# Pooled attention and a gelu MLP on one core: a weight sum, K's spread, an operand sum and a query load put elsewhere in a hand-written order

## The chip, the cores and the metric

The kernel runs on one core of a Trainium2 chip. The metric is the device time of one execution in microseconds (us), as the median of several. Five engines work side by side: TensorE (PE in the profile, with PEld for its weight loads), VectorE (DVE), ScalarE (ACT), GpSimd (POOL) and SyncE (SP), which here only issues DMAs. Each takes its instructions in the order in which the program gives them, so an instruction that waits holds up everything behind it on its engine.

## The reference

Attention over pooled keys and values, and then an MLP with gelu:

```python
B, H, S, D = q.shape                      # 8, 8, 576, 64
k_p = k.reshape(B, H, S // 8, 8, D).mean(axis=3)     # 72 keys a head
v_p = v.reshape(B, H, S // 8, 8, D).mean(axis=3)
scores = scale * np.matmul(q, k_p.transpose(0, 1, 3, 2))
attn = np.exp(scores - np.max(scores, axis=-1, keepdims=True))
attn = attn / (np.sum(attn, axis=-1, keepdims=True) + 1e-09)
x = np.matmul(attn, v_p)                  # then transposed to (B*S, H*D) = (4608, 512)
h = x @ w_in                              # 512 -> 2048
g = 0.5 * h * (1.0 + np.tanh(c * (h + 0.044715 * h * h * h)))
out = g @ w_out                           # 2048 -> 512
```

## The kernel before, in words

The 4608 rows are worked in nine groups of 512. Eight groups are the first 512 queries of a batch each; the ninth, called R (the remainder), gathers the last 64 queries of all eight batches. The order is `seq` = 0, 1, ..., 6, R, 7, and a group's turn is called a step here, numbered by its place in `seq`: step 7 is R, step 8 is batch 7.

A step is the MLP of its group on TensorE. Into the same stretch the attention of the next group is woven, and the loads of the one after. Step 0 has its own form, `mlp_first`. In the others `mlp` makes the hidden layer in 64 places (0 to 63; `hidden_two` at L526 and `hidden` at L379 in steps 1 and 2, and from step 3 on, where `fast` is true, `hidden_fast`, a product of Strassen's kind at L470), and then the output layer at L581 as seven half-size products in the order 1, 2, 6, 5, 7, 3, 4, with 16 matmuls each, in places 64 to 175. Product n in this order starts at place 64 + 16n.

The weaving is by hand. `at(hooks, s, f, ...)` puts a call on a list for place s, and `hook(s)` makes all calls of place s just ahead of the matmul of that place. So a call's place fixes where its instructions stand in each engine's queue; when they run depends on what they wait for. Calls of one place are made in the order in which they were put there.

The parts that the change touches:

- `w_sums` (L423): four sums of pieces of `w_out`, made once into `tw` by VectorE, 128x2048 each. Number 0 stands at place 185 of step 0, numbers 1 to 3 in the first places of step 1. Products 5, 6, 7 and 4 use them.
- `values` (L338, for R L349): the product of weights and V, and the casts of its result to `xT`, the input of the next step's hidden layer. It stands late in every step, at place 186 in step 0. In step 0 and step 1 two casts of 128x1024 are made, one by ScalarE and one by VectorE.
- `g_sums` (L430 to L434): sums of blocks of the gelu output `gT`. Its lines L430 to L432 (which 0) make s3, a block in place, and s2; L434 (which 1) makes s4, the fourth operand. Product 6 reads s2, product 7 s3, product 3 s4.
- `k_spread` (L94 through `copy`, written `kbd<-kTd`): two copies of the transposed, pooled K of the next group into `kbd`, which the scores (L244) read. `spread_v` (L172, `vbd`) does the like for V on GpSimd.
- `norm` (L260, L269, L275) makes the softmax weights `eb` from the exponentials, j = 0 and 2 on GpSimd and j = 1 and 3 on VectorE, and `e_transpose_dma` (L302) turns each of the four into `eT` by a DMA issued on SP. `values` reads `eT`: its first eight matmuls of a batch step need j = 0 and 1, the next need j = 2 and 3.
- `load_q` loads queries on SP. A batch is one DMA (L121, 1 MB). R's are gathered from all batches by eight DMAs of 128 KB (L125), in rows of 64 floats, four for `(0, 2)` and four for `(2, 4)`. The tile `q_sb` has two buffers in turn. `cast_gated` casts it on GpSimd, two steps ahead of the queries' own step.
- `load_kv` loads K and V of a group (L112, L107, L105: 2.25 MB in four DMAs, from place 28 of a step on).

Everything that SP issues stands in one queue: loads, transposes and the stores of the output (L411).

Of the kernel before, what the change touches and what calls it, by code (L numbers as in the profile page):

```python
# [19 lines left out]
def kernel(  # L20
# [21 lines left out]
    nc = tc.nc  # L42
# [10 lines left out]
    R = B  # L53
    seq = list(range(B - 1)) + [R, B - 1]
# [20 lines left out]
    NP = FO // 2  # L75
# [534 lines left out]
    def mlp_first(g, hooks):  # L610

        hook = runner(hooks)
        s = 0
        for half, c in [(0, 0), (0, 1), (0, 2), (1, 0), (0, 3), (1, 1), (1, 2), (1, 3)]:
            for fo in range(4 * c, 4 * c + 4, 2):
                hidden_half(g, fo, half, hook, s)
                s += 8
        nc.scalar.preload_act_table_set(EXP_SET)
        o = [psum.tile([128, DM], F32, name="mm", tag="mm", bufs=4) for _ in range(4)]
        for fo in range(12):  # L620
            for r in range(4):
                hook(s)
                s += 1
                output(g, r, fo, o[r])
        for r in range(4):
            for fo in range(12, FO):
                hook(s)
                s += 1
                output(g, r, fo, o[r])
            finish(g, r, o[r], nc.scalar if r == 3 else nc.vector)  # L630
        assert not hooks, sorted(hooks)
# [134 lines left out]
    def at(hooks, s, f, *a):  # L766
        hooks.setdefault(s, []).append(lambda: f(*a))

    def tail_of_attention(hooks, n, va):
        at(hooks, va, xT_tile, n)  # L770
        at(hooks, va, nc.scalar.preload_act_table_set, GELU_SET)
        at(hooks, va, values, n, False)

    hooks = {}
# [40 lines left out]
    at(hooks, 156, load_q, 2, 0, 4, nc.sync)  # L815
    at(hooks, 156, load_main, 2, "v", 0, 4, nc.sync)
    tail_of_attention(hooks, 1, 186)
    at(hooks, 185, w_sums, 0, 0, NP, nc.vector)
    mlp_first(0, hooks)

    for n_, g in enumerate(seq):
        if n_ == 0:
            continue
        hooks = {}
        fast = n_ >= 3
        if n_ == 1:
            for i in range(1, 4):
                at(hooks, i, w_sums, i, 0, NP, nc.vector)
            at(hooks, 36, g_sums, 0, 4)
            at(hooks, 57, g_sums, 4, 6)  # L830
        elif fast:
            at(hooks, 41, g_sums, 0, 2, (0,))
            at(hooks, 57, g_sums, 2, 6, (0,))
            at(hooks, 65, g_sums, 6, 8, (0,))
            at(hooks, 64 + 32, g_sums, 0, 8, (1,))
        else:
            at(hooks, 20, g_sums, 0, 2)
            at(hooks, 36, g_sums, 2, 4)
            at(hooks, 57, g_sums, 4, 6)
        if not fast:  # L840
            at(hooks, 65, g_sums, 6, 8, (0,))
            at(hooks, 64 + 32, g_sums, 6, 8, (1,))
        if n_ + 1 < len(seq):
            n = seq[n_ + 1]
            b = B - 1 if n == R else n
            kv = n != B - 1
            if n_ == 1:
                for j in range(4):
                    at(hooks, 22 + 4 * j, cast_q, n, j, j + 1, nc.scalar)
                at(hooks, 35, qT_tile, n)  # L850
                at(hooks, 35, q_transpose_dma, n)
            if kv and not fast:
                t0 = 22 if n_ == 1 else 12
                at(hooks, t0, pool, b, 0, 5)
                at(hooks, t0, dup_k, b, 0, 5)
                at(hooks, t0, kT_tile, b, None)
                at(hooks, t0, k_transpose_dma, b)
                t1 = t0 + (16 if n_ == 1 else 24)
                at(hooks, t1, pool, b, 5, 9)
                at(hooks, t1, spread_v, b, nc.gpsimd)  # L860
                at(hooks, 56, k_spread, b, [nc.vector, nc.vector])
            elif kv:
                at(hooks, 5, pool, b, 0, 5, (0,))
                at(hooks, 17, pool, b, 0, 5, (1,))
                at(hooks, 17, dup_k, b, 0, 5)
                at(hooks, 17, kT_tile, b, None)
                at(hooks, 17, k_transpose_dma, b)
                at(hooks, 17, spread_gated, b)
                at(hooks, 40, k_spread, b, [nc.gpsimd, nc.gpsimd])
            if fast:  # L870
                at(hooks, 2, qT_tile, n)
                at(hooks, 2, q_transpose_dma, n)
            sc_at = [68, 68, 90, 90]
            for j in range(4):
                at(hooks, sc_at[j], scores, n, j)
                at(hooks, sc_at[j] + 1, exps, n, j)
            at(hooks, 80, eT_tile, n)
            for j in range(4):
                at(hooks, 80 if j < 2 else 92, norm, n, j, nc.vector if j % 2 else nc.gpsimd)
                at(hooks, 80 if j < 2 else 92, e_transpose_dma, n, j)  # L880
            at(hooks, 64 + 66, nc.scalar.preload_act_table_set, GELU_SET)
            va = 64 + (102 if n_ > 1 else 100)
            at(hooks, va, xT_tile, n)
            at(hooks, va, values, n, n_ > 1)
        if n_ + 2 < len(seq):
            n2 = seq[n_ + 2]
            s2 = 44 if n_ == 1 else 8 if n2 == R else 57
            at(hooks, s2, q_tile, n2)
            if n2 == R:
                at(hooks, s2, load_q, n2, 0, 2, nc.sync)  # L890
                at(hooks, 30, load_q, n2, 2, 4, nc.sync)
            else:
                at(hooks, s2, load_q, n2, 0, 4, nc.sync)
            at(hooks, 64 + 52, cast_gated, n2)
            if n_ < 2:
                at(hooks, 64 + 100, qT_tile, n2)
                at(hooks, 64 + 100, q_transpose_dma, n2)
                at(hooks, 64 + 100, load_kv, n2, (1,))
            elif n2 != B - 1:
                b2 = B - 1 if n2 == R else n2  # L900
                at(hooks, 64 + 84, pool, b2, 5, 9, (0,))
                at(hooks, 64 + 97, pool, b2, 5, 9, (1,))
            if n_ == 1:
                at(hooks, 45, load_kv, n2, (0,))
            else:
                at(hooks, 28, load_kv, n2)
        mlp(g, hooks, n_ + 1 == len(seq), fast)
# [30 lines left out]
```

## Time and profile before

| | |
|---|---|
| Median of 8 runs | 281.6 us (280.33 to 282.18) |
| Profiled execution: time, span of the core | 281.94 us, 280.2 us |
| Granted TensorE clock | 1.000 |
| Busy: TensorE, weight loads | 269.7 us (96%), 191.9 us (68%) |
| Busy: VectorE, ScalarE, GpSimd | 224.8 us (80%), 175.7 us (63%), 71.8 us (26%) |
| DMA | 54.37 MB, 71696 packets |
| First matmul of steps 1 to 8 | 53.14, 82.55, 110.86, 138.52, 166.32, 195.54, 223.84, 251.39 us |

The times in a profile's rows are microseconds from the start of the span. A row of the timeline gives start, duration, engine, line of the kernel, operation, the tiles written and read, their shapes, and how many instructions were merged into it; in brackets stands how long the engine was idle ahead of it, and what ended that. Matmuls are pipelined: what a group of them takes is best read from the start of the first to the start of what comes next.

### The profile page before, as it was taken

The numbers are of one execution on the slowest core, as the hardware profiler recorded it, in microseconds if no ns is written. First come the engines' busy times: TensorE is split into PE (matmuls) and PEld (weight loads), VectorE is DVE, ScalarE is ACT, GpSimd is POOL, SyncE is SP. The second block draws the span as 40 slices with busy tenths as digits, with TensorE's granted clock in tenths as the row PEclk, the third lists the DMA queues.
The fourth block names the chain that finished last, engine by engine and source line by source line (L and its number), as shares of the span: only waits on it lengthen the run. The fifth ranks groups of instructions, "written<-read, shape, count | busy, mean of one in ns | idle before, by whom it ended". The sixth has DMA issues, their size and how long they took to land.

```text
span 280.2 us, 6562 instructions
## 1 busy us (share of the span) xinstructions
PE 269.7 (96%) x2686; PEld 191.9 (68%) x2686; DVE 224.8 (80%) x365; ACT 175.7 (63%) x263; POOL 71.8 (26%) x108
## 2 busy tenths in 40 slices
PE   7989999899989999999999999998999999999995
PEld 3668844346854588668766876686668876886684
DVE  5886969999956988988998999898988658865832
ACT  1586576398627765696479637962696478656820
POOL 4640172003410333223331433242133400300000
PEclk9999999999999999999999999999999999999999
DMA  7999999998989895899479969995752460243013
GB/s 223 309 196 291 371 386 202 300 352 234 232 190 247 259 272 141 173 297 238 124 173 279 266 122 215 236 227 150 163 162 49 124 150 2 46 94 108 1 41 112
DMA packets 71696, 54.37 MB, mean 194 GB/s; under 512 B 45554, under 2 KB 57842, under 8 KB 71666
## 3 DMA queue, kind: packets, MB, share of 16 engines
q1 hardware_dynamic: 69410, 51.72, 72.2%
q0 software_dynamic: 2112, 2.10, 4.6%
q8 instruction: 21, 0.34, 0.5%
q10 hardware_dynamic: 144, 0.13, 0.1%
q14 instruction: 9, 0.07, 0.1%
HBM read 36.70 MB, written 9.44 MB: 165 GB/s over the span
## 4 chain that ended last, share of the span: by engine, by line
PE 71%; DVE 14%; DMA 8%; SPq 3%; ACT 2%; issue 1%; POOL 0%; DVEq 0%; ACTq 0%; POOLq 0%
PE mm L581 24%; PE mm L379 21%; PE c L470 11%; DMA q_sb<-in_q_dram 5%; PE mm L390 5%; PE x L581 2%; DVE den L260 2%; DVE eb L275 2%; PE xo L338 2%; DMA eT<-eb 2%; PE sc L244 1%; DVE kv L149 1%; PE mm L526 1%; SPq L125 1%; DMA out_dram<-osb 1%
## 5 line engine op out<-in xcount | busy, mean ns | idle before, releaser
L379 PE MATMUL mm<-xT,w_in_b 128*128 128x512 bf16 x304 | 69.9, 379 | 0.0
L581 PEld LDWEIGHTS <-gT 128*128 128x128 bf16 x512 | 48.4, 98 | 8.8 <-issue 1.2
L381 ACT ACTIVATE gT<-mm 128x512 bf16<-128x512 f32 x76 | 43.9, 598 | 15.4 <-PE mm L379 14.9
L379 PEld LDWEIGHTS <-w_in_b 128*128 128x128 bf16 x304 | 29.8, 98 | 30.7
L581 PEld LDWEIGHTS <-stage 128*128 128x128 bf16 x384 | 37.2, 98 | 5.7 <-DVE stage L434 1.4
L275 POOL TENSOR_TENSOR eb<-e,r 128x576 bf16<-128x576 f32 x14 | 16.1, 1149 | 65.3 <-DVE r L269 50.2
L92 ACT CAST xT<-xo 128x512 bf16<-128x512 f32 (+1 forms) x22 | 12.6, 631 | 31.0 <-PE xo L338 26.4
L172 POOL TENSOR_TENSOR vbd<-kvb,vmask 128x256 bf16<-128x256 bf16 (+2 forms) x38 | 21.2, 582 | 39.1 <-DVE kvb L152 24.5
L260 DVE TENSOR_REDUCE den<-e 128x8 f32<-128x576 f32 x36 | 26.2, 728 | 5.6 <-ACT e L253 5.6
L581 PE MATMUL mm<-w_out_b,gT 128*128 128x256 bf16 x240 | 29.9, 273 | 0.0
L581 PE MATMUL mm<-tw,gT 128*128 128x256 bf16 x240 | 29.9, 273 | 0.0
L253 ACT ACTIVATE e<-sc 128x576 f32<-128x576 f32 x36 | 22.5, 650 | 7.7 <-POOL eb L275 5.8
L92 ACT COPY osb<-mm 128x512 f32<-128x512 f32 x30 | 17.8, 592 | 14.5 <-PE mm L581 13.9
L581 PE MATMUL mm<-tw,stage 128*128 128x256 bf16 x224 | 26.7, 273 | 0.0
L149 DVE TENSOR_TENSOR kv<-kv 128x1024 f32<-128x1024 f32 (+3 forms) x19 | 23.5, 1236 | 3.6 <-DMA kv<-in_k_dram 2.5
L470 PEld LDWEIGHTS <-ws 128*128 128x128 bf16 x192 | 18.8, 98 | 6.0
L94 POOL CAST q_b<-q_sb 128x1024 bf16<-128x1024 f32 (+1 forms) x15 | 15.1, 1026 | 19.5 <-PE mm L390 14.2
L275 DVE TENSOR_TENSOR eb<-e,r 128x576 bf16<-128x576 f32 x18 | 18.3, 1015 | 0.6
L470 PE MATMUL c<-tt,ws 128*128 128x256 bf16 x144 | 17.7, 273 | 0.0
L430 DVE TENSOR_TENSOR stage<-gT 128x512 bf16<-128x512 bf16 (+1 forms) x25 | 13.0, 519 | 3.8 <-ACT gT L486 2.0
L390 PE MATMUL mm<-xT,w_in_b 128*128 128x256 bf16 x128 | 15.6, 273 | 0.1
L431 DVE TENSOR_TENSOR gT<-gT 128x512 bf16<-128x512 bf16 (+1 forms) x25 | 13.0, 522 | 3.0 <-ACT gT L381 1.2
(106 smaller groups left out, 408.5 us busy)
## 6 DMA issues: line engine op xcount, KB each, us to landing
kv<-in_k_dram SPq DMA_DIRECT2D x7, 1024.0 KB, 6.8
q_sb<-in_q_dram SPq DMA_DIRECT2D x7, 1024.0 KB, 9.8
kv<-in_v_dram SPq DMA_DIRECT2D x6, 1024.0 KB, 8.7
out_dram<-osb SPq DMA_DIRECT2D x12, 512.0 KB, 3.1
out_dram<-osb SPq DMA_DIRECT2D x11, 256.0 KB, 3.3
kv<-in_v_dram SPq DMA_DIRECT2D x4, 512.0 KB, 10.4
w_in_b<-in_moe_w_in_dram POOLq DMA_DIRECT2D x4, 512.0 KB, 6.7
w_out_s<-in_moe_w_out_dram SPq DMA_DIRECT2D x2, 1024.0 KB, 13.7
```

The lines of the kernel that those rows point to most:

```text
L92: eng.copy(out=out, in_=in_)
L94: eng.tensor_copy(out=out, in_=in_)
L149: add(out=t[:, :, 0:4, :], in0=t[:, :, 0:4, :], in1=t[:, :, 4:8, :], op=ALU.add)
L172: eng.tensor_tensor(out=vbd[p0:128, b, n0:n1, :].rearrange("p (c r) (hh d) -> p c (r hh) d", c=max(m, 1), d=D), in0=kvb[p0:128, 4 + c0:4 + ...
L253: nc.scalar.activation(out=e.rearrange("p (x h) s -> p x (h s)", x=2), in_=sc[:, :, 0:4 * Sp], func=ACT.Exp, scale=1.0 / 64.0)
L260: nc.vector.reduce_sum(out=den, in_=e, axis=AX.X)
L275: eng.tensor_tensor(out=o.rearrange("p (pr hh s) -> p hh pr s", hh=2, s=Sp), in0=e.rearrange("p (hh pr) s -> p hh pr s", hh=2), in1=r.rear ...
L379: nc.tensor.matmul(out=hp, lhsT=w_in_b[:, ko, fo * 128:(fo + 1) * 128], rhs=st[g]["xT"][:, ko, :], start=(i == 0), stop=(i == KO - 1))
L381: nc.scalar.activation(out=gT[:, fo, :], in_=hp, func=ACT.Gelu_apprx_tanh)
L390: nc.tensor.matmul(out=hp[:, f, :], lhsT=w_in_b[:, ko, (fo + f) * 128:(fo + f + 1) * 128], rhs=st[g]["xT"][:, ko, c0:c0 + 256], start=(ko ...
L470: nc.tensor.matmul(out=acc[:, m, :], lhsT=lhs(i, m), rhs=rhs(i), start=bool(fresh and i == 0 and m % 2 == 0), stop=(i == 1), skip_group_ch ...
L581: nc.tensor.matmul(out=xs[p] if acc is xs else acc[:, p, :], lhsT=lt, rhs=rt, start=bool(fresh and m == 0 and (p == 0 or (last and acc is ...
```

## The change

Four things are placed differently; no arithmetic is added.

1. Weight sum 0 moves from place 185 to place 187 of step 0, that is, from ahead of `values` to behind it.
2. In steps 1 and 2 `k_spread` moves from place 56 on VectorE to GpSimd, at place 38 or 36, behind the pooling of V and ahead of `spread_v`.
3. The fourth operand sum (L434) is made in two halves: in steps 3 to 8 its blocks 0 to 3 at place 65 and 4 to 7 at place 96, where all eight stood at 96. In steps 1 and 2 blocks 4 and 5 move from place 57 to 96, to stand in one instruction with 6 and 7.
4. R's first four query DMAs move from step 5, place 8, to step 4, place 58, just behind the load of batch 6's queries. The last four move from place 30 of step 5 to place 8.

```diff
@@ step 0
-    at(hooks, 185, w_sums, 0, 0, NP, nc.vector)
+    at(hooks, 187, w_sums, 0, 0, NP, nc.vector)
@@ n_ == 1
-            at(hooks, 57, g_sums, 4, 6)
+            at(hooks, 57, g_sums, 4, 6, (0,))
         elif fast:
...
-            at(hooks, 64 + 32, g_sums, 0, 8, (1,))
+            at(hooks, 65, g_sums, 0, 4, (1,))
         else:
...
-            at(hooks, 57, g_sums, 4, 6)
+            at(hooks, 57, g_sums, 4, 6, (0,))
         if not fast:
             at(hooks, 65, g_sums, 6, 8, (0,))
-            at(hooks, 64 + 32, g_sums, 6, 8, (1,))
+        at(hooks, 64 + 32, g_sums, 4, 8, (1,))
@@ if kv and not fast
                 at(hooks, t1, pool, b, 5, 9)
+                at(hooks, t1, k_spread, b, [nc.gpsimd, nc.gpsimd])
                 at(hooks, t1, spread_v, b, nc.gpsimd)
-                at(hooks, 56, k_spread, b, [nc.vector, nc.vector])
@@ if n_ + 2 < len(seq)
-            s2 = 44 if n_ == 1 else 8 if n2 == R else 57
-            at(hooks, s2, q_tile, n2)
+            s2 = 44 if n_ == 1 else 57
             if n2 == R:
-                at(hooks, s2, load_q, n2, 0, 2, nc.sync)
-                at(hooks, 30, load_q, n2, 2, 4, nc.sync)
+                at(hooks, 8, load_q, n2, 2, 4, nc.sync)
             else:
+                at(hooks, s2, q_tile, n2)
                 at(hooks, s2, load_q, n2, 0, 4, nc.sync)
+            if n_ + 3 < len(seq) and seq[n_ + 3] == R:
+                at(hooks, s2 + 1, q_tile, R)
+                at(hooks, s2 + 1, load_q, R, 0, 2, nc.sync)
```

## The prediction

> **What bounds the kernel now.** I read the page's busy shares first, then TensorE's waits, then the timeline around each wait.
>
> ```profile
> PE 269.7 (96%) x2686; PEld 191.9 (68%) x2686; DVE 224.8 (80%) x365; ACT 175.7 (63%) x263; POOL 71.8 (26%) x108
> PE xo L338 <- DMA eT<-eb: 2.2, 2, 1.4
> PE mm L526 <- DVE xT L94: 1.0, 1, 1.0
> PEld L581 <- DVE stage L434: 1.4, 5, 0.3
> ```
>
> TensorE (PE) sets the end. No part of the change touches a matmul, so it can gain only what TensorE now waits, and these rows are the waits of the steady part. The last three rows are: waited for, us in total, times, longest. Each is looked up in the timeline (start, duration, engine, line).
>
> End of step 0:
>
> ```profile
> 49.54 1.28 DVE L94 COPY osb<-mm 128x512 f32<-128x512 f32 x2
> 50.74 1.21 DVE L423 TENSOR_TENSOR tw<-w_out_b 128x2048 bf16<-128x2048 bf16 x1
> 51.87 1.21 DVE L94 CAST xT<-xo 128x1024 bf16<-128x1024 f32 x1
> 53.14 1.04 PE L526 MATMUL mm<-xT,w_in_b 128*128 128x512 bf16 x4 [0.99 <-DVE xT L94]
> ```
>
> The weight sum stands in VectorE's (DVE's) queue ahead of the xT cast, and TensorE waits 0.99 for the cast.
>
> Step 5, where a product of 16 matmuls normally takes 1.75 from start to start:
>
> ```profile
> 187.31 1.91 PE L581 MATMUL mm<-tw,stage 128*128 128x256 bf16 x16
> 187.98 1.21 DVE L434 TENSOR_TENSOR stage<-gT,stage 128x2048 bf16<-128x2048 bf16 x1
> 189.25 1.64 PEld L581 LDWEIGHTS <-stage 128*128 128x128 bf16 x16 [0.31 <-DVE stage L434]
> 191.75 0.41 PE L338 MATMUL xo<-eT,vbd 32*64 32x256 bf16 x8
> 193.53 0.97 PE L338 MATMUL xo<-eT,vbd 32*64 32x256 bf16 x24 [1.37 <-DMA eT<-eb]
> ```
>
> Product 7 takes 189.25 - 187.31 = 1.94, so 0.19 is lost to the fourth operand sum. The value matmuls take 2.68 here (191.75 to the next product at 194.44) against 1.12 in step 3: 1.56 lost to the last transpose of the weights eT. The same sums over the other steps: product 7 loses 0.19 in steps 3, 4, 5 and 6 and 0.10 in step 7; the values lose 1.0 in step 1 (2.19 against 1.18 in step 2) and 0.15 in step 4.
>
> What SyncE (SP) issues ahead of those transposes, and what the DMA engines then move:
>
> ```profile
> 148.39 0.51 SPq L121 DMA_DIRECT2D q_sb<-in_q_dram  x1
> 156.80 6.08 SPq L302 DMA_TRANSPOSE eT<-eb  x4
> 163.95 1.34 PE L338 MATMUL xo<-eT,vbd 32*64 32x256 bf16 x32
> 178.08 5.43 SPq L125 DMA_DIRECT2D q_sb<-in_q_dram  x4
> 184.61 7.51 SPq L302 DMA_TRANSPOSE eT<-eb  x4
> 178.00:180.00 2.00, 2.00 (x25) 1.01 (x27) 1.84 (x3) 1.98 (x5) 1.01 (x2) 1.00 1.03 397
> 184.00:189.00 5.00, 5.00 (x48) 4.44 (x46) 4.79 (x8) 2.71 (x4) 2.61 (x3) 1.00 1.44 188
> 149.00:158.00 9.00, 9.00 (x128) 6.56 (x127) 7.61 (x14) 7.61 (x13) 1.15 (x1) 1.00 1.06 334
> ```
>
> In the last three rows the last two columns are DMA share and GB/s. In step 5 the four late queries of the remainder fill the queue in front of the eT transposes. Step 4 (148 to 164) is just as full without them: DMA share over 1 for nine us, and its values already wait a little.
>
> **The change part by part**, against the profiled execution's own 281.94 (span 280.2 and 1.7 around it; the median shown is 281.6, 0.34 less).
>
> *Weight sum behind the cast.* No instruction is added. The two values casts start once the value matmuls end (about 50.75); two osb copies end at 50.82. The cast then runs about 50.8 to 52.0 and TensorE, free at 52.15, does not wait: -0.99. The osb copy that frees the next accumulator comes third as before and ends about 53.75; TensorE wants that bank at 54.88 - 0.99 = 53.89. Cover 0.14; without it at most 0.1 comes back. The sum itself is used 20 us later, in product 5 of step 1.
>
> *K spread by GpSimd, and L434 later, steps 1 and 2.* Step 1 loses 1.0 because VectorE is behind: its first den starts at 70.37, 0.7 after its input. Moved off it: the two kbd copies (65.69 to 66.65, 0.96 with gaps) and one L434 of 0.42. On GpSimd (POOL) the copies stand in front of spread_v, wait for the K transpose (issued 60.27, page 3.3 us for this kind, so about 63.6), and cost 2 x 0.42 (median of the eight that GpSimd does in later steps). spread_v's remaining parts wait anyway for V, pooled at 65.77; the scores want kbd at 66.5. Cover about 1.5. Against it: VectorE's kv addition L149 of 128x1024 takes 1.22 at 63.38, and 1.96 at 162.51 beside the q_b cast on GpSimd. The Trainium skill, "GPSIMD Engine Reference", section 1 (Specifications), says that GpSimd shares its SBUF interfaces with VectorE and contends with VectorE instructions that have two SBUF inputs, which is this addition. Charged in full, the rule gives back 0.84 of the 1.38; by the rows 0.74 per 1.45 of overlap, so 0.4 to 0.5. I take the rows. L431 at 61.31 waits 0.30 for a gelu that now comes earlier, so den starts 0.96 + 0.42 + 0.3 - 0.45 = 1.2 to 1.7 (no contention) earlier, and the transposes behind it, issued one after another in 6.07 and landing 2.6 later, with it. TensorE itself arrives 0.99 earlier, so of the step's wait only 0.2 to 0.7 goes: I take -0.3. Ends: +0.8 (the transposes land hardly earlier and step 0's gain is swallowed here), and -0.9. In step 2 VectorE waits for the exponentials already (gap 0.52), and nothing is gained: 0. Its transposes land at 108.81 against a use at about 109.0, so 0.2 could be lost.
>
> *Fourth sum in two halves, steps 3 to 8.* 1.21 becomes 2 x 0.69. The first half goes ahead of the den reductions, into a gap of 0.58 (step 4) or 0.47 (step 5): den is 0.14 to 0.24 later, and so are the norms and transposes queued behind. The second half then ends 0.3 earlier than the whole did, enough for the 0.19: -0.19 in steps 3 and 6, -0.10 in step 7 (their last transposes land 0.7 before use: 135.91 against 136.67 in step 3). In steps 4 and 5 the transpose is last anyway and this gain is swallowed: 0. In step 8 product 7 loses nothing now: 0.
>
> *Remainder's queries.* Step 5 keeps four DMAs at hook 8 and loses the four at 178.08. Transposes behind 2.25 MB of K and V alone should follow steps 3 and 4, 6.8 to 7.5 from first issue to last landing: 184.85 + 7.3 = 192.1, so 1.4 of the 1.56 and 0.19 comes back: -1.4 (ends -1.7, -1.0). Step 4 gains four DMAs, each 0.64 of SP time, 0.52 MB together, right behind q6 (lands 148.39 + 11.85 = 160.24) and ahead of the eT transposes. SP had 7.9 us free there, but in step 5 the third and fourth took 1.94 and 2.09 with only K and V in front, and here q6's 1 MB stands there besides. Price by the row: 0.52 MB at the 188 GB/s of 184 to 189, 2.8 us; so they land at 163.0. In step 5 the last eT landed 3.66 after the last query (193.49 - 189.83): 166.7 here, against 164.27 before: +2.4. The Trainium skill, "DMA: Bandwidth & Descriptors", "Why small descriptors are slow (HBM only)", gives 11 cycles for the 8 of a 256-byte piece, the size of a remainder query row: 397 x 8/11 = 289 GB/s, 1.8 us, and +1.4. Rule and row both speak against this edit; the row is the same transfer, so it weighs more. I take +2.0 (ends 0, if SP places all four before the queue fills and they slip in, and +3.0).
>
> Sum: -0.99 - 0.3 - 0.19 + 2.0 - 1.4 - 0.19 - 0.10 = -1.2 (rounded). 281.94 - 1.2 = 280.7 for an execution like the profiled one, 280.4 for the median.
>
> **The rivals.**
>
> *A. The queries cost nothing in step 4.* For it: SP's 7.9 free us, and a wait of only 0.15 there now. Against it: DMA share 1.06 from 149 to 158. Then +2.0 becomes about +0.2: sum -3.0, 278.6.
>
> *B. The front gains are swallowed.* Step 1's last transpose lands when it did, at 80.1, because its issue chain is held by transfers, not by VectorE: -0.99 and -0.3 become -0.2. Sum -0.1: 281.5. For it: the second transpose of that step took SP 2.12 instead of 1.23. Against it: the first was issued as soon as its weights were there (72.66).
>
> *C. Slower: the queue in step 4.* If SP is held for every one of the four DMAs as it was for the last two in step 5 (about 2 us each), the first eT transpose leaves at about 158.4 and the last lands at 158.4 + 8.9 = 167.3 or later, and the next store and qT transpose follow late. It decides above +4.1 in step 4, where the sum passes about +0.85 (-3.2 + 4.1); with 4.5 it is +1.3: 282.9. Against it: those 2 us holds hide partly in SP's free time.
>
> *D. The edit does not do what it says.* The order of instructions shows all four moves, so only the wait on a buffer could undo one: the remainder's query buffer is that of step 5's queries, cast a step earlier. I give this nothing.
>
> **How the numbers follow.** Main case 0.48 (279.4 to 281.3, its centre 280.4), A 0.22, B 0.18, C 0.12. A measurement of this kernel can tell about 0.3%, 0.85 us, from no change: faster is below 280.75. Of the main case 0.36 lies there, of A all, of B 0.01: 0.59. Same: 0.11 of the main case and 0.17 of B, 0.01 of C: 0.29. Slower: the rest, 0.12. The range runs from A's centre to between B and C: 278.5 to 282.0.
>
> **What would show it.** Right: no wait of L526 on xT at 52; L338 in step 1 at about 1.9; product 7 at 1.75 in steps 3 to 7; L338 in step 5 near 1.2; and L338 in step 4 at about 3 with queries landing near 163 less the shift. A is right if step 4's L338 stays under 1.6; B if step 1's stays over 2.8; C if step 4's is over 5. I am wrong at the root if TensorE shows a wait in a step and for a tile not named here.

## The result, and the profile after

The changed kernel takes 284.7 us (median of 11 runs, 283.1 to 286.2) against 281.7 for the kernel before in the same measurement: a ratio of 1.0111, interval 1.0092 to 1.0131. It is slower, by 3.0 us; the forecast was 280.4, in a range that ended at 282.0. The profiled execution took 284.15 us, its span is 282.4 (before: 281.94 and 280.2), so the two traces show 2.2 of the 3.0.

The page of the kernel after, its first line of busy times, the granted clock, and the shares of the chain that ended last:

```profile
PE 271.0 (96%) x2686; PEld 193.2 (68%) x2686; DVE 223.6 (79%) x365; ACT 175.4 (62%) x263; POOL 74.1 (26%) x112
...
PEclk9999999999999999999999979999999999999999
...
PE 59%; DVE 16%; DMA 15%; ACT 3%; SPq 3%; issue 2%; POOL 1%; DVEq 0%; ACTq 0%
```

TensorE is busy 1.3 us longer with the same 2686 matmuls, and one slice of 40 has a lower clock (7 tenths, at 162 to 169). In the chain, DMA has 15% and TensorE 59%, where it was 8% and 71%: more of the time now runs through transfers. TensorE's waits in the kernel after (waited for: us in total, times, longest):

```profile
PE xo L338 <- DMA eT<-eb: 4.5, 3, 2.1
...
PE sc L244 <- DMA qT<-q_b: 0.2, 1, 0.2
```

The waits of L526 on `xT` and of L581 on the fourth sum are gone, as intended. The wait on `eT` has doubled, and there is a small new one on `qT` in step 1. The timeline around the places that the prediction showed, first the end of step 0:

```profile
49.44 1.28 DVE L94 COPY osb<-mm 128x512 f32<-128x512 f32 x2
...
50.70 1.22 DVE L94 CAST xT<-xo 128x1024 bf16<-128x1024 f32 x1
51.85 1.21 DVE L423 TENSOR_TENSOR tw<-w_out_b 128x2048 bf16<-128x2048 bf16 x1
...
51.99 1.90 PE L526 MATMUL mm<-xT,w_in_b 128*128 128x512 bf16 x8
```

The cast now stands ahead of the weight sum, and L526 starts at 51.99 (53.14 before) with no idle time ahead of it. Step 5:

```profile
191.18 1.91 PE L581 MATMUL mm<-tw,stage 128*128 128x256 bf16 x16
...
192.42 0.68 DVE L434 TENSOR_TENSOR stage<-gT,stage 128x1024 bf16<-128x1024 bf16 x1
192.92 1.91 PE L581 MATMUL mm<-w_out_b,stage 128*128 128x256 bf16 x16
...
195.42 0.81 PE L338 MATMUL xo<-eT,vbd 32*64 32x256 bf16 x12
```

Product 7 takes 192.92 - 191.18 = 1.74, and the value matmuls 1.41 instead of 2.68 (195.42 to the next product at 196.83). All that was forecast there came. Step 4 is where the time went (first SP's queue, then TensorE):

```profile
146.95 0.53 SPq L121 DMA_DIRECT2D q_sb<-in_q_dram  x1
147.53 9.66 SPq L125 DMA_DIRECT2D q_sb<-in_q_dram  x4
157.30 8.02 SPq L302 DMA_TRANSPOSE eT<-eb  x4
...
161.67 0.82 PE L581 MATMUL mm<-tw,gT 128*128 128x256 bf16 x6
...
164.21 0.41 PE L338 MATMUL xo<-eT,vbd 32*64 32x256 bf16 x8 [1.72 <-DMA eT<-eb]
...
166.73 1.64 PE L338 MATMUL xo<-eT,vbd 32*64 32x256 bf16 x24 [2.11 <-DMA eT<-eb]
...
168.29 2.06 PE L581 MATMUL mm<-tw,gT 128*128 128x256 bf16 x10
```

The four query DMAs hold SP for 9.66, until 157.2. The last `eT` lands at 166.68. From 161.67, TensorE needs 8.52 us to the end of the ten matmuls at 170.19; before, the same took 3.12 (163.20 to 166.32). The step loses 5.40.

The windows of the kernel after at the end of that wait (from and to, length; then busy us and count of PE, PEld, DVE, ACT, POOL; granted clock; DMA share; GB/s):

```profile
166.00:167.00 1.00, 0.27 (x8) 0.18 (x8) 0.00 (x0) 0.00 (x0) 0.00 (x0) 0.77 0.66 219
167.00:168.00 1.00, 1.00 (x24) 0.55 (x16) 0.00 (x0) 0.01 (x1) 0.00 (x0) 0.50 0.81 328
...
169.00:170.00 1.00, 1.00 (x7) 0.70 (x6) 0.55 (x2) 0.55 (x2) 0.00 (x0) 0.52 0.00 0
170.00:171.00 1.00, 1.00 (x11) 0.90 (x10) 0.97 (x3) 0.58 (x1) 0.00 (x0) 1.00 0.00 0
```

After the two waits the clock is at half for 3.41 us (166.54 to 169.96). This is a second loss on top of the waiting: the 24 value matmuls take 1.56 from start to start instead of 0.84, the ten of the product 1.89 instead of 1.10, together 1.5.

Step by step, from the starts of TensorE's groups in the two traces (where TensorE stands against before; minus is earlier):

| | shift | what made it |
|---|---|---|
| first product of step 1 | -1.16 | the `xT` wait (0.99); the rest is within what the traces differ by |
| start of step 2 | -1.07 | +0.30 `qT` wait, -0.21 `eT` wait |
| step 4, product 4 | -1.53 | product 7 in steps 3 and 4, 0.19 each; rest small |
| end of step 4 | +3.87 | +5.40 in step 4 |
| after step 5's values | +2.4 | product 7 -0.19, values -1.27 |
| last product | +2.16 | product 7 in steps 6 and 7 |

The first row is less sure than it looks. Traces of kernels that are alike up to step 1 begin that step at different times: its hidden layer begins at 52.25 to 53.14 with the weight sum ahead of the cast, and at 51.31 to 51.99 with it behind.

### The profile page after: what moved, and what is told of

The parts are those of the page before. It is cut to its first block, busy times and chain, and to the rows that moved or that the text cites. A ratio compares the mean times of both kernels' runs of the same rounds, so it can differ in the third digit from the quotient of the medians.

```text
span 282.4 us, 6567 instructions
## 1 busy us (share of the span) xinstructions
PE 271.0 (96%) x2686; PEld 193.2 (68%) x2686; DVE 223.6 (79%) x365; ACT 175.4 (62%) x263; POOL 74.1 (26%) x112
## 3 DMA queue, kind: packets, MB, share of 16 engines
q0 software_dynamic: 2112, 2.10, 4.7%
## 4 chain that ended last, share of the span: by engine, by line
PE 59%; DVE 16%; DMA 15%; ACT 3%; SPq 3%; issue 2%; POOL 1%; DVEq 0%; ACTq 0%
PE mm L581 20%; PE mm L379 14%; PE c L470 11%; DMA q_sb<-in_q_dram 10%; PE mm L390 5%; DVE den L260 3%; DVE eb L275 3%; DMA eT<-eb 3%; PE x L581 2%; PE xo L338 2%; DMA qT<-q_b 2%; ACT gT L486 1%; DVE kv L149 1%; PE sc L244 1%; POOL q_b L94 1%
## 5 line engine op out<-in xcount | busy, mean ns | idle before, releaser
L581 PEld LDWEIGHTS <-gT 128*128 128x128 bf16 x512 | 48.8, 99 | 9.4 <-issue 1.4
L381 ACT ACTIVATE gT<-mm 128x512 bf16<-128x512 f32 x76 | 43.5, 598 | 14.5 <-PE mm L379 14.2
L581 PEld LDWEIGHTS <-stage 128*128 128x128 bf16 x384 | 37.6, 98 | 4.3
L581 PE MATMUL mm<-tw,gT 128*128 128x256 bf16 x240 | 30.7, 277 | 0.0
L581 PE MATMUL mm<-w_out_b,gT 128*128 128x256 bf16 x240 | 29.9, 273 | 0.0
L92 ACT COPY osb<-mm 128x512 f32<-128x512 f32 x30 | 17.8, 592 | 14.8 <-PE mm L581 14.2
L581 PE MATMUL mm<-tw,stage 128*128 128x256 bf16 x224 | 26.7, 273 | 0.0
L149 DVE TENSOR_TENSOR kv<-kv 128x1024 f32<-128x1024 f32 (+3 forms) x19 | 22.9, 1204 | 3.7 <-DMA kv<-in_k_dram 2.5
L172 POOL TENSOR_TENSOR vbd<-kvb,vmask 128x256 bf16<-128x256 bf16 (+2 forms) x38 | 21.9, 598 | 7.4 <-DVE kvb L152 6.3
L94 POOL CAST q_b<-q_sb 128x1024 bf16<-128x1024 f32 (+1 forms) x15 | 16.6, 1127 | 19.9 <-DMA q_sb<-in_q_dram 19.9
L430 DVE TENSOR_TENSOR stage<-gT 128x512 bf16<-128x512 bf16 (+1 forms) x25 | 13.4, 536 | 4.1 <-ACT gT L381 2.0
L94 DVE CAST xT<-xo 128x512 bf16<-128x512 f32 (+1 forms) x10 | 8.0, 795 | 10.6 <-PE xo L338 7.4
```

The lines of the kernel that those rows point to most:

```text
L92: eng.copy(out=out, in_=in_)
L94: eng.tensor_copy(out=out, in_=in_)
L149: add(out=t[:, :, 0:4, :], in0=t[:, :, 0:4, :], in1=t[:, :, 4:8, :], op=ALU.add)
L172: eng.tensor_tensor(out=vbd[p0:128, b, n0:n1, :].rearrange("p (c r) (hh d) -> p c (r hh) d", c=max(m, 1), d=D), in0=kvb[p0:128, 4 + c0:4 + ...
L381: nc.scalar.activation(out=gT[:, fo, :], in_=hp, func=ACT.Gelu_apprx_tanh)
L581: nc.tensor.matmul(out=xs[p] if acc is xs else acc[:, p, :], lhsT=lt, rhs=rt, start=bool(fresh and m == 0 and (p == 0 or (last and acc is ...
```

## The experiments

They ran in three groups, each with its own runs of the kernel before on the same chip (medians 281.61, 281.03 and 281.5). Every ratio is to those.

**Theory:** the four query DMAs at place 58 of step 4 put 0.5 MB ahead of the `eT` transposes on DMA engines that have no room, and all of the loss comes from there. **Rivals:** SP's queue order alone (the transposes are issued late because SP is held), the small pieces of 256 bytes, the clock after the idle time, or one of the other three parts.

### Parts 1 to 3 without the queries, and the queries alone

```diff
e1: the changed kernel, with the query code of before
-            s2 = 44 if n_ == 1 else 57
+            s2 = 44 if n_ == 1 else 8 if n2 == R else 57
...
e2: the kernel before, with part 4 of the change alone
-                at(hooks, s2, load_q, n2, 0, 2, nc.sync)
-                at(hooks, 30, load_q, n2, 2, 4, nc.sync)
+                at(hooks, 8, load_q, n2, 2, 4, nc.sync)
...
+                at(hooks, s2 + 1, load_q, R, 0, 2, nc.sync)
```

> The change without its fourth part: the remainder's eight query DMAs stay in step 5 as before. Theory Q (the four query DMAs in step 4 fill SP's queue, hold the transposes of eT and let TensorE idle until its clock falls): the other three parts keep the gain that the profile of the changed kernel shows up to place 96 of step 4 (shift -1.5), and two more products 7 without a wait, so 279.6 to 280.2, about 1.7 below the kernel before. Rival S (the earlier place of TensorE, or K's spread on GpSimd, shifts the loads of steps 1 to 4 into each other, and the queries only happen to stand there): still above the kernel before, 282 to 284.

> The kernel before with the fourth part alone. Theory Q: step 4's value matmuls and the product around them lose 4 to 5.5 us, step 5 gives back 1.3 to 1.6, so +3 to +4: 284.7 to 285.7. Rival S: the query DMAs alone are nearly free without the shift of the other parts, 281 to 282.5.

Parts 1 to 3: 280.33, ratio 0.9965 (0.9944 to 0.9985), 1.3 us faster. The queries alone: 285.82, ratio 1.015 (1.0128 to 1.0172), 4.2 us slower. -1.3 + 4.2 = 2.9, which is the change's 3.0: the two halves add up, and the loss belongs to the queries. The timeline of step 4 without the queries, from e1:

```profile
146.78 0.51 SPq L121 DMA_DIRECT2D q_sb<-in_q_dram  x1
155.30 5.70 SPq L302 DMA_TRANSPOSE eT<-eb  x4
162.25 1.19 PE L338 MATMUL xo<-eT,vbd 32*64 32x256 bf16 x32
```

and with the queries alone, from e2:

```profile
148.34 9.76 SPq L125 DMA_DIRECT2D q_sb<-in_q_dram  x4
158.21 7.97 SPq L302 DMA_TRANSPOSE eT<-eb  x4
165.08 0.41 PE L338 MATMUL xo<-eT,vbd 32*64 32x256 bf16 x8 [1.68 <-DMA eT<-eb]
...
167.60 1.25 PE L338 MATMUL xo<-eT,vbd 32*64 32x256 bf16 x24 [2.11 <-DMA eT<-eb]
```

In e1 step 4's values follow without a wait. In e2 they wait the same 1.7 and 2.1 as in the changed kernel. e1 is also the base against which the changed kernel's transfers must be read, since TensorE stands nearly alike in both (product 4 begins at 161.50 and 161.67): its last `eT` lands at 162.37, the changed kernel's at 166.68.

### The same four DMAs at another time: e3, and a part of them: e12

```diff
e3: all four at place 8 of step 4 instead of 58
-                at(hooks, s2 + 1, load_q, R, 0, 2, nc.sync)
+                at(hooks, 8, load_q, R, 0, 2, nc.sync)
e12: two at place 8, two at place 58
+                at(hooks, 8, load_q, R, 0, 1, nc.sync)
+                at(hooks, s2 + 1, load_q, R, 1, 2, nc.sync)
```

> The changed kernel, but the remainder's first four query DMAs in step 4 at place 8, ahead of the loads of K and V, instead of place 58 behind batch 6's queries. The bytes of the two steps are the same. If the place behind a full queue is what costs (theory Q): SP takes 0.6 us for each, as in step 5, K and V of step 4 go out 2 to 3 us later, and the last eT lands 0 to 2 us later than in the kernel before; total 279 to 281.5. If the bytes of step 4 alone cost (3.75 MB ahead of the transposes, whatever the order): as the changed kernel, 284 to 285.

> The changed kernel with two of the remainder's four early query DMAs behind batch 6's queries (place 58 of step 4) and two at place 8. Dose against the 0 and 4 already run: there the last eT of step 4 landed at 162.4 and 166.7. If what counts is the transfer ahead of the transposes, half of it: 164 to 165, step 4's values lose about 2, the clock stays at 1.0[...], and the time is 281 to 282.5. If two are held no longer than none because the queue only then fills: 162.4 to 163.2, 279.5 to 280.5.

e3: 279.97, ratio 0.9944 (0.9922 to 0.9966). e12: 280.76, ratio 0.997 (0.9953 to 0.9988). e12 came under the 281 to 282.5 that were expected, though its `eT` lands where it was expected. The timeline of e3 and then that of e12:

```profile
141.53 2.70 SPq L125 DMA_DIRECT2D q_sb<-in_q_dram  x4
...
155.12 5.99 SPq L302 DMA_TRANSPOSE eT<-eb  x4
...
163.10 0.97 PE L338 MATMUL xo<-eT,vbd 32*64 32x256 bf16 x24 [0.56 <-DMA eT<-eb]
```

```profile
142.28 1.35 SPq L125 DMA_DIRECT2D q_sb<-in_q_dram  x2
...
148.03 4.40 SPq L125 DMA_DIRECT2D q_sb<-in_q_dram  x2
155.89 7.36 SPq L302 DMA_TRANSPOSE eT<-eb  x4
...
163.93 0.41 PE L338 MATMUL xo<-eT,vbd 32*64 32x256 bf16 x8 [1.03 <-DMA eT<-eb]
...
164.91 0.97 PE L338 MATMUL xo<-eT,vbd 32*64 32x256 bf16 x24 [0.57 <-DMA eT<-eb]
```

Six us earlier, ahead of K, V and batch 6's queries, the same four DMAs hold SP for 2.70 instead of 9.66, and the last `eT` lands at 163.05. Of e12's pairs the early one holds SP for 1.35, the late one for 4.40. With none, two or four of them at place 58 the last `eT` lands 15.6, 17.4 and 19.7 after the issue of batch 6's queries (162.37 - 146.78, 164.87 - 147.49, 166.68 - 146.95): 1.8 for the first pair and 2.3 for the second. TensorE loses about 0, 1.7 and 5.4; the last is so much larger partly because only there the clock drops too (it is 1.000 throughout e12's profiled execution).

### Is it SP's queue? e5

```diff
-                at(hooks, s2 + 1, load_q, R, 0, 2, nc.sync)
+                at(hooks, s2 + 1, load_q, R, 0, 2, nc.gpsimd)
```

> The changed kernel with the four query DMAs of step 4 issued by GpSimd on its own queue instead of by SP, at the same place 58. If what costs is that they stand in SP's queue ahead of the eT transposes and hold it (each took SP 2.0 to 2.7 us, the first transpose then 4.06): the transposes leave as in the kernel without the queries, step 4's value matmuls take 1.1 to 2.0, the clock stays, and the time is 279.5 to 281. If what costs is 0.5 MB more on the same DMA engines: the last eT still lands 1.5 to 2.4 us late, 282.5 to 284.5.

284.97, ratio 1.0137 (1.0108 to 1.0165): no better, and above even the 282.5 to 284.5 that were expected if the bytes are what costs. Its timeline:

```profile
147.07 2.80 POOL L125 DMA_DIRECT2D q_sb<-in_q_dram  x4
147.07 0.51 SPq L121 DMA_DIRECT2D q_sb<-in_q_dram  x1
155.55 9.85 SPq L302 DMA_TRANSPOSE eT<-eb  x4
...
166.27 0.64 PE L338 MATMUL xo<-eT,vbd 32*64 32x256 bf16 x8 [3.70 <-DMA eT<-eb]
```

With the queries out of SP's queue, SP is free when `eb` is ready and issues the first transpose at 155.55. That one goes in 1.33, but the next three hold SP for 3.58, 2.43 and 2.23, and the last lands at 167.28. The queries themselves land early (154.9 to 159.6) and push back what was ahead of them on SP: V takes 13.4 from issue to landing, and batch 6's queries 15.7, landing at 162.81. TensorE waits 3.70 in one piece, and its clock is then at half for 6.83, twice as long as in the changed kernel. So SP's order only decides which transfer is late. The bytes are the same on the same DMA engines. The Trainium skill, "DMA: Bandwidth & Descriptors", "Issuing engines are not separate DMA queues", says just this, that DMAs of any issuing engine run on the same 16 DMA engines and interleave; the trace agrees. One thing besides the queue differs in e5: its profile counts 192 packets for these queries, where SP's were 2112, so the pieces are not the same.

### The small pieces, or the bytes? e6

e6 loads the same amount, 0.5 MB in four DMAs, at place 58, but in rows of 4 KB from another part of `q`, which R's own queries overwrite later; R's own first half comes in step 5. Only step 4 is read from it.

```diff
+    def load_long(i):
+        nc.sync.dma_start(out=st[R]["q"][32 * i:32 * i + 32].rearrange("p h j d -> p (h j d)")[:, 0:1024],
+                          in_=q[0].rearrange("h s d -> (h s d)")[32768 * i:32768 * i + 32768].rearrange("(p f) -> p f", f=1024))
...
-                at(hooks, s2 + 1, load_q, R, 0, 2, nc.sync)
+                for i in range(4):
+                    at(hooks, s2 + 1, load_long, i)
```

> The changed kernel, but the four DMAs at place 58 of step 4 carry the same 0.5 MB in rows of 4 KB (of another part of q, overwritten later), and the remainder's first half is loaded with the second in eight DMAs at place 8 of step 5. Only step 4 is read. If the number of pieces fills the queue (2048 of 256 bytes against 128 or 256 long ones): SP takes 0.6 us for each DMA, the first eT transpose 1.2, and step 4's value matmuls 1.1 to 2.2. If the bytes do it: SP is held about as long as in the changed kernel, and the value matmuls lose over 2 us. The total is not read, since step 5 has more to load: 280 to 284.

285.1 (ratio 1.0145, 1.0109 to 1.0182), with step 5 loaded more than in the changed kernel. The rows of its query DMAs and its transposes (duration ns: least, median, longest; first and last start):

```profile
L129 SPq DMA_DIRECT2D q_sb<-in_q_dram x4: 416/420/2582, 147.7 to 151.2; - x4
L306 SPq DMA_TRANSPOSE eT<-eb x4: 1216/1673/2629, 155.7 to 161.2; - x4
```

Only the first long-row DMA holds SP (2.58); the others go in 0.42. The first transpose leaves at 155.65, but the last still lands at 165.27. Counted from the issue of batch 6's queries as above, that is 18.1, against 15.6 without and 19.7 with the small pieces: the bytes cost 2.5 and the small pieces 1.6 more. The query DMAs themselves say the same: the last lands 14.2 after that issue with long rows and 15.0 with small pieces, where batch 6's queries alone (e1) land after 11.4. So 0.52 MB add 2.8 and 3.6. The bytes are the larger part.

### The clock: e4 and e10

Idle matmuls on zeros were put ahead of step 4's values, so that TensorE isn't idle in the wait: 30 matmuls of 256 columns in e4, and 128 of 48 columns in e10, which makes TensorE's program 256 instructions longer than the changed kernel's.

```diff
+        if g == 5:
+            for _ in range(30):
+                nc.tensor.matmul(out=xo[0][:, 0, :], lhsT=zeros, rhs=zeros.unsqueeze(1).to_broadcast([128, 2, 128]),
+                                 start=True, stop=True, skip_group_check=True)
```

> The changed kernel with 30 idle matmuls of 256 columns on zeros (3.3 us) in front of the value matmuls of step 4, inside the 3.8 us in which TensorE waits there. If the clock of 0.5 that followed the wait is a consequence of the idle time, the clock stays at 1.0, the 24 value matmuls and the 10 after them take 0.8 and 1.1 instead of 1.56 and 1.89, and the time falls by 1 to 1.6 to 283.1 to 283.7. If the clock falls for another reason, the time stays at 284.7 or grows by up to 0.3.

> As the kernel with 30 idle matmuls, but with 128 small ones (48 columns, 64 weights columns), so that TensorE's program grows by 256 instructions, 16 KB, the size of one of its code loads, and later code loads fall where they fell in the changed kernel. If the 2.3 us that the first filled kernel lost again in steps 6 and 8 came from code loads colliding with stores: they are gone, and the time is 282.9 to 283.6. If they came from the earlier place of steps 6 to 8: 284.3 to 284.9 again. The clock should stay at 1.0.

e4: 284.59, ratio 1.0104 (1.0083 to 1.0125). e10: 284.24, ratio 1.0116 (1.0075 to 1.0157). The windows of e4 in the same columns as above, and its wait in step 8:

```profile
166.00:167.00 1.00, 0.23 (x8) 0.14 (x8) 0.00 (x0) 0.00 (x0) 0.00 (x0) 1.00 0.70 229
167.00:168.00 1.00, 1.00 (x27) 0.67 (x20) 0.18 (x1) 0.43 (x1) 0.00 (x0) 1.00 0.81 328
```

```profile
PE c L474 <- ACT osb L499: 1.1, 1, 1.1
```

The clock stays at 1.00, and the ten matmuls of the product take 1.10 again. The mean clock is 0.999 or 1.000 in all six executions of e4, and 0.994 or 0.988 in all twelve of the changed kernel. TensorE is 1.4 ahead of the changed kernel by step 5. So the clock's drop comes from the idle time, and is worth 1.4 at that place. But the time of the whole is not better: in e4 the gain is lost again in steps 6 and 8 (0.7 and 1.6). In step 8 TensorE waits for a copy by ScalarE, which began late behind a store that took 4.83 to land instead of 3.25. In e10 those two losses are absent (step 5's values wait 0.9 there instead) and the profiled execution is 0.8 shorter than the changed kernel's, yet the medians, against their own runs of before, show no gain that their intervals can tell. Why the gain isn't kept in the medians stays open. Expectation missed.

### The other three parts, each alone on the kernel before: e7, e8, e9

```diff
e7: part 1
-    at(hooks, 185, w_sums, 0, 0, NP, nc.vector)
+    at(hooks, 187, w_sums, 0, 0, NP, nc.vector)
e8: part 2
+                at(hooks, t1, k_spread, b, [nc.gpsimd, nc.gpsimd])
-                at(hooks, 56, k_spread, b, [nc.vector, nc.vector])
e9: part 3
-            at(hooks, 64 + 32, g_sums, 0, 8, (1,))
+            at(hooks, 65, g_sums, 0, 4, (1,))
...
+        at(hooks, 64 + 32, g_sums, 4, 8, (1,))
```

> The kernel before with the first part alone (weight sum behind the xT cast in step 0). By the prediction's step: no wait of L526 on xT, -0.99, of which step 1 takes back some because its transposes then are needed earlier and VectorE is not relieved: 0.0 to -0.9 at the end, 280.7 to 281.6. By the rival that front gains are swallowed in step 1: no difference at the start of step 2, 281.4 to 281.8.

> The kernel before with the second part alone (K of steps 1 and 2 spread by GpSimd). VectorE's den of step 1 starts 0.7 earlier, where its exponentials limit it, and the values of step 1 wait 0.3 to 0.7 less: -0.3 to -0.7, 280.9 to 281.4. If the transposes of step 1 are held by transfers and not by VectorE: 0, 281.6.

> The kernel before with the third part alone (fourth operand sum in two halves, and L434 of steps 1 and 2 at place 96). Product 7 takes 1.75 instead of 1.94 in steps 3 to 6 and 1.84 in step 7; where the transposes come last anyway (step 5, and a little step 4) it is swallowed: -0.5 to -0.7 at the end, 281.0. If den, now 0.14 to 0.24 later, brings the transposes late: 281.5 to 281.9.

The weight sum alone: 281.37, ratio 0.999 (0.9973 to 1.0007), nothing that can be told. K's spread alone: 281.29, 0.999 (0.9971 to 1.0009), likewise. The fourth sum alone: 280.4, 0.9962 (0.9944 to 0.9981), faster. TensorE's waits in e7:

```profile
PE xo L338 <- DMA eT<-eb: 3.5, 5, 1.5
...
PE sc L244 <- DMA qT<-q_b: 0.4, 1, 0.4
```

The profiled execution of e7 is the slowest of its fourteen (282.65), so its trace shows where the gain can go rather than what the median did. In it step 0 gains 1.36, and all of it is given back: 0.52 at the scores of step 1, which wait for `qT`, and 0.58 each at the values of steps 1 and 2, which wait longer for `eT`. TensorE comes earlier, but what it needs next doesn't. In e8 and e9 the values of step 1 take 0.35 and 0.66 less: both free VectorE ahead of the softmax of step 1 (e9 because L434 of blocks 4 and 5 leaves place 57). With all three parts, TensorE stands 1.7 earlier at the start of step 2 in e1, 1.07 in the changed kernel, and with part 3 alone 0.97 in e9. By the medians part 3 alone (0.9962) gives as much as the three together (0.9965). That parts 1 and 2 add anything to it is not shown.

### Loads in pairs where there is room: e11

The experiments point to R's eight DMAs in places ahead of K and V or behind the transposes. e11 is the changed kernel with a pair in each of four places:

```diff
-                at(hooks, 8, load_q, n2, 2, 4, nc.sync)
+                at(hooks, 8, load_q, n2, 3, 4, nc.sync)
...
+            if n_ == 3:
+                at(hooks, 150, q_tile, R)
+                at(hooks, 150, load_q, R, 0, 1, nc.sync)
+            if n_ == 4:
+                at(hooks, 8, load_q, R, 1, 2, nc.sync)
+                at(hooks, 150, load_q, R, 2, 3, nc.sync)
```

> The changed kernel with the remainder's eight query DMAs in four pairs, each where SP and the DMA engines have room: place 150 of step 3 (behind the eT transposes), place 8 and place 150 of step 4, place 8 of step 5. If a pair costs nothing there: no value matmuls above 1.3 in steps 4 and 5, and 278.4 to 279.2. If pairs behind the transposes hold the stores and through them the next step's ScalarE copies: 279.5 to 280.5, no better than with four DMAs at place 8 of steps 4 and 5.

278.9 (278.5 to 279.88), ratio 0.9928 (0.9902 to 0.9954). It has the lowest ratio here, 0.7% ahead of before and 1.8% ahead of the changed kernel (0.9928 / 1.0111 = 0.982); its interval overlaps that of e3 (0.9922 to 0.9966), so pairs are not shown to be better than fours at place 8. The row of its query DMAs, and the largest steady waits of its TensorE:

```profile
L125 SPq DMA_DIRECT2D q_sb<-in_q_dram x8: 617/626/664, 133.3 to 170.2; - x8
```

```profile
PE xo L338 <- DMA eT<-eb: 0.6, 1, 0.6
PE sc L244 <- DMA qT<-q_b: 0.5, 1, 0.5
```

No query DMA holds SP for more than 0.66. Step 4's values take 1.45, a little over the 1.3 expected, and step 5's 1.12: the gain of step 5 without the price in step 4.

## Why the prediction was wrong, point by point

*Weight sum (-0.99).* The start of step 1's first product moved by -1.16, and no cover failed. Right at that place, though alone it gains nothing that can be told (e7).

*K's spread and L434 in step 1 (-0.3).* The values of step 1 gained 0.21, but a wait on `qT` of 0.30 appeared ahead of the scores, which the prediction did not name (its last sign of being wrong, on a small scale): `qT` landed at 66.36 before and at 66.60 after, while TensorE came 1.16 earlier. Net +0.1, so steps 0 and 1 gave -1.07 at the start of step 2 where -1.3 was forecast. GpSimd's copies waited for the K transpose until 65.00, not 63.6, so L149 was over before them and took 1.22 as before. The contention came at other lines: L152 took 0.53 beside the copies (0.42 before), and L432 and the second L430 took 0.72 and 0.83 beside `spread_v`, which now runs later (0.50 and 0.42 before). So the first `den` came 0.84 earlier (69.53 against 70.37), where 1.2 to 1.7 were forecast. The charge of 0.4 to 0.5 was too small: some 0.6 was lost in this stretch (VectorE was 0.18 ahead at L149, 0.96 and 0.35 were moved off it, and 0.84 was left). It rested on a misreading. The cast on GpSimd ended at 163.39 and L149 began at 162.51, so they overlap 0.88, not 1.45; 0.74 per 0.88 makes 0.7 for the 0.84 of copies.

*Fourth sum (-0.19, -0.19, -0.10).* Right: 1.75 in each of steps 3 to 7.

*Queries leaving step 5 (-1.4).* Right in size: -1.27, and -0.19 at product 7.

*Queries coming to step 4 (+2.0): the step that failed.* The price in `eT` had the mechanism and the place of the prediction, but not the size, and the drop of the clock behind it was not in the prediction at all. Measured is +5.40. The term, rebuilt from the traces:

| | us |
|---|---|
| the row's price in the prediction (2.0 was chosen, between rule and row) | 2.4 |
| queries land at 161.96; 163.0 less the 1.44 by which batch 6's queries were issued earlier is 161.56 | +0.4 |
| last `eT` 4.72 behind the last query, where 3.66 was taken from step 5 | +1.06 |
| the base: TensorE needs it at 162.70 (161.67 + 0.75 + 0.28), where 164.27 less 1.44 is 162.83 | +0.13 |
| TensorE's clock at half behind the idle time: 0.72 (1.56 - 0.84) and 0.79 | +1.51 |
| sum, with 0.05 from landing to start, less the 0.15 that the step lost before already | 5.4 |

The choice between rule and row went the wrong way. The row's 2.8 for the transfer was short by 0.4, and the rule's 1.8 by 1.4: measured from batch 6's queries as they landed before, 160.24 - 1.44 = 158.80, the last query comes 3.16 later. That it lands only 2.08 behind them (159.88) says nothing, since it has pushed them back as well. What the Trainium skill, "DMA: Bandwidth & Descriptors", "Why small descriptors are slow (HBM only)", says of small pieces was not the fault (3.6 against 2.8 in e6 is 1.3 times as long, the rule's 11/8 is 1.4), but the 397 GB/s that it was applied to: in e6 even 4-KB rows came at 0.52 MB in 2.8 us, 187 GB/s.

Then the 3.66 of step 5 was carried over. When the last query landed there (189.83), the third of the four transposes was just being issued, here (161.96) the second. One more is one more step of 1.31 in the chain. The row for L302 in the changed kernel shows it:

```profile
L302 SPq DMA_TRANSPOSE eT<-eb x4: 1217/1228/4063, 157.3 to 164.1; - x4
```

The first is held 4.06, to 161.37, and the other three follow 1.31 apart (start to start), with 2.59 from the last issue to landing: 161.46 + 2 x 1.31 + 2.59 = 166.7. And nothing in the prediction asked what an idle TensorE does to its clock: in the profiled execution before, no wait in the steady part was longer than 1.4, and the granted clock was 1.000 throughout. (In 7 of the 99 later executions of the kernel before it was 0.994, and these took 283.5 to 284.9.)

*The rivals.* C, at 0.12, was the one that came, though its 282.9 was short as well, in good part by the clock: it had SP held about 2 us for each of the four DMAs, and measured are 2.45, 2.66, 1.96 and 2.46. Its first transpose at 158.4 and last landing at 167.3, less the 1.44, are 157.0 and 165.9; measured are 157.30 and 166.68. It was discounted since "those 2 us holds hide partly in SP's free time". They did hide: SP was free until about 155.3 (e1), so the first transpose left only 2.0 late. But e5 shows that the loss comes without the queries' hold on SP, too. The engines behind it were full (DMA share 1.08 from 149 to 158 without the queries, in e1, and 1.10 with them), so that what is added there delays the rest, whoever issues it. Once the queries have landed, the engines are no longer full (0.66 from 163.13 to 166.54): the last part of the wait is the chain of the transposes, which SP sends one after another. The row against rival A, DMA share 1.06, was thus the row that should have priced the step, not only decided that there is a price. B was wrong for the three parts together, and right for part 1 alone. D was nothing.

*The sum.* The other terms came nearly as forecast; +5.4 in place of +2.0 makes +2.2 in the traces, where -1.2 was written. The medians differ by 3.0, which the two single traces don't show in full. A part of the rest is the clock: three of the eleven executions have a mean clock of 0.988 and not 0.994, and they are the slowest (285.8 to 286.2); the other eight have a median of 284.2. e1 and e2, each with its medians, give 2.9.

## What to carry to other kernels

Where the DMA engines' share stands at 1 until the transfers that the bound engine waits for, look for another place for added bytes: here 0.52 MB delayed the last of these transfers by 4.3 us (166.68 against 162.37), another issuing queue didn't help (167.28), and half the load cost TensorE less than half (1.7 against 5.4, e12). Put the load where there is room. Price such a move at the last transfer that the bound engine needs, with its own chain behind the load (here four transposes 1.31 apart), and add the price of idleness: waits that leave TensorE little work in some 3.4 us cost it its clock as well, 1.5 here. And a wait removed ahead of a transfer that nothing has made earlier is only moved to that transfer (e7).

## What the runs showed of the hardware that was not expected

- TensorE's granted clock fell to 0.50 at 166.54, after a stretch of 4.2 us (162.49 to 166.73) in which it worked 0.41, and was 1.00 again at 169.96. The stretch at half is 3.41 long in the changed kernel, e2 and e6, and 6.83 in e5. In all four the stretch at 1.00 ahead of it is a whole multiple of 3.413 (160.43 = 47 x 3.413, in e2 163.84 = 48 x 3.413). So in these traces the clock changes in steps of one window of 3.41. The windows below are such steps, in the columns as above: one of the changed kernel, two of e6 and two of e7.

```profile
163.13:166.54 3.41, 0.41 (x8) 0.17 (x8) 0.78 (x2) 0.00 (x0) 0.00 (x0) 1.00 0.66 132
```

```profile
162.71:166.13 3.42, 1.22 (x32) 0.68 (x32) 1.47 (x3) 0.01 (x1) 0.50 (x1) 1.00 0.79 224
166.13:169.54 3.41, 3.41 (x24) 2.30 (x17) 2.48 (x4) 2.14 (x4) 0.00 (x0) 0.50 0.00 0
```

```profile
192.10:195.52 3.42, 1.88 (x39) 0.99 (x37) 2.57 (x5) 0.47 (x1) 0.00 (x0) 1.00 0.70 212
195.52:198.90 3.38, 3.33 (x29) 2.65 (x28) 2.69 (x5) 2.59 (x5) 0.00 (x0) 1.00 0.31 120
```

The clock fell behind windows with 0.41, 0.96 (e2), 0.00 (e5) and 1.22 us (e6) of matmuls. It did not behind one with 1.88 (e7). In e6 TensorE waited only 1.67 and 0.57, so no single long wait is needed; in e12 waits of 1.03 and 0.57 left 2.30 in the window and the clock at 1.000. The Trainium skill, "TensorE: Matmul & The Clock Gate", Part 1, gives one idle window of about 3.4 us as the condition, in windows that run on their own. The traces agree on the length, with the addition that a window with a third of its time in work still lowered the clock.
- A 128 KB DMA in 512 pieces held SP for 0.62 to 0.67 where the engines had room (e3, e11), and for 2.0 to 2.7 behind 3.25 MB of K, V and queries; the same bytes in 32 rows of 4 KB took 0.42 there, but for the first (2.58).
- The same four query DMAs issued by GpSimd overtook what SP had issued before them: they took 7.8 to 10.5 us to land, while V, issued ahead of them, took 13.4.
